# Order of the second maximum, the first sums and the outer stretches of values in a decode attention kernel

## The chip, the cores and the metric

The kernel runs on one core of a Trainium2 chip. The metric is the time of one execution on the device in microseconds (us). Before the change three runs took 639.89, 640.02 and 637.45 us; their median is 639.89. A separate execution was taken with the hardware profiler.

## What is computed

Grouped-query attention for a single query position: 32 query heads share 8 key/value heads (4 each), with 65536 keys of 128 numbers, all bf16.

```python
B, Hq, Hkv, Sq, Sk, D = 1, 32, 8, 1, 65536, 128
scores = jnp.einsum("bhqd,bhkd->bhqk", q, k) * scale
p = _softmax(scores, axis=-1)
return jnp.einsum("bhqk,bhkd->bhqd", p, v)
```

K and V are 134 MB each and every element is used once, so the kernel has to bring 268 MB into the core.

## The kernel before, in words

**Rounds.** The keys of one head are cut into two rounds of 32768 keys; 8 heads make 16 rounds (`NR`). A round's keys lie as 128 partitions times 256 rows: a "row" is a tile of 128 keys by 128 numbers. K of a round goes to `kbuf`, V to `vbuf`, each by one large transfer of 8 MB on SP's queue (`load_both`, L466). `kbuf` has room for 352 rows, so that the next round's keys can be written where this round's first part has been used up; `vbuf` holds one round.

**Parts.** Each round is worked on in two parts, a first part of 160 rows (`A`) and a second of 96 (`C`). Each part has a running maximum of its own, so there are 32 parts with indices `u`; `u % 2` tells first from second. In even rounds the first part is rows 0 to 160; in odd rounds it is rows 96 to 256 (`row_tile`, L63), so that the rows used first are those which the next load overwrites first.

**One round, engine by engine.**
- TensorE (`pe_keys`, L162) transposes the keys in blocks of 8 rows (L136) and multiplies each transposed block with the 4 queries (L155). The first part's scores go to two PSUM banks, the second part's to a third. The second part's transposes stand twice in the code, once for even and once for odd rounds, behind branches (L168, L171). Then `pe_values` (L181) multiplies the exponentials with V (L178) in three stretches of rows: 96 to 160 (stretch 1, in the first part of every round), 0 to 96 (stretch 0) and 160 to 256 (stretch 2). They are run in the order 1, 0, 2 with one wait for the semaphore `exd` ahead of stretch 1 (first part's exponentials) and one ahead of stretch 0 (second part's). The last round has code of its own (`pe_last`, L192), where the first part's 160 values stand ahead of the second wait.
- VectorE (`dve_round`, L321) and ScalarE share the copies of the transposed blocks from PSUM to `ktb` (L240, L238). VectorE then reduces the scores to a maximum per query (L260), GpSimd takes it over the partitions (L438), VectorE joins it with the running maximum (`maximum`, L276: `m`, `dm`, `negm`), and ScalarE computes the exponentials with their sums (`exponentials`, L390). `add_sums` (L287) adds these sums to `lp`; it waits for ScalarE (`sx`). In `dve_round` the first part's `add_sums` stands ahead of the second part's reduction.
- `add_values` (L307) waits for `pvd`, which TensorE sends with the last value, gives `vbuf` free (`vfree`), and adds the three stretches to `acc`.
- SP (`sync_engine`, L446) waits for `kfree`, queues the next K, waits for `vfree`, queues the next V. `kfree` comes from VectorE with the copy of the first part's last block (L236). All transfers are on one queue.

**The ends.** Up to round 13 K and V come in one transfer each, but for round 0's K in three. Round 14's K and V come in two (160 and 96 rows), round 15's K in three (64, 96 and 96 rows), each with a semaphore of its own (`krdy`), and round 15's V in eight: 96 and 64 rows for the first part, then 48, 24, 12, 6, 4 and 2 rows (`V_PIECES`) for the second. In `pe_last` a small matmul (L206) stands between the 48th and the 49th value of the second part and waits for VectorE's sums (`t_lp`, L377).

TensorE's program is a loop over the rounds (L222) whose start is aligned to a block of 256 instructions.

Of the kernel before, what the change touches and what calls it, by code (L numbers as in the profile page):

```python
# [5 lines left out]
DT = mybir.dt  # L6
AF = mybir.ActivationFunctionType
ALU = mybir.AluOpType
AX = mybir.AxisListType

P = 128


T = 128
C = 96
A = 2 * T - C
# [25 lines left out]
def take(e, sem, n=1):  # L42

    e.wait_ge(sem, n)
    e.sem_inc(sem, -n)  # L45


def bass_standalone__gqa_softmax__decode_kernel(nc, q, k, v, out):
    _, Hq, _, D = q.shape
    _, H, Sk, _ = k.shape  # L50
    R = Hq // H
# [3 lines left out]
    scale = float(D) ** -0.5  # L55
# [7 lines left out]
    def row_tile(odd, x):  # L63
        return (x + C) % (2 * T) if odd else x
# [6 lines left out]
    def sb(name, shape, dt):  # L71
        return S(nc.sbuf_tensor(name, shape, dt))

    def sem(name):
        return S(nc.semaphore(name))
# [14 lines left out]
    cmax = [sb(f"cmax{i}", [P, R], DT.float32) for i in range(2)]  # L90
    cmaxa = sb("cmaxa", [P, R], DT.float32)
    m = [sb(f"m{i}", [P, R], DT.float32) for i in range(2)]
    dm = sb("dm", [P, R], DT.float32)
    negm = sb("negm", [P, R], DT.float32)
    alpha = [sb(f"alpha{i}", [P, R], DT.float32) for i in range(2)]
    rsum = [sb(f"rsum{i}", [P, R], DT.float32) for i in range(2)]
    acc = sb("acc", [P, R], DT.float32)[:, :]
    lp = sb("lp", [P, R], DT.float32)
    la = sb("la", [P, R], DT.float32)
# [10 lines left out]
    pvb = S(nc.psum_tensor("pvb", [P, BANK], DT.float32))  # L110
# [3 lines left out]
    vrdy = [sem(f"vrdy{i}") for i in range(2)]  # L114
# [3 lines left out]
    qkd, qrdy, pvd = sem("qkd"), sem("qrdy"), sem("pvd")  # L118
    cm, cma, ng, exd, sx, lrd, lra = (sem(n) for n in ("cm", "cma", "ng", "exd", "sx", "lrd", "lra"))
    xd, xa, xg = sem("xd"), sem("xa"), sem("xg")  # L120
# [56 lines left out]
    def value(pe, out, r, first, last):  # L177
        return pe.matmul(out, lhsT=vbuf[:, r * D:(r + 1) * D], rhs=pts[:, r * R:(r + 1) * R],  # L178
                         start=first, stop=last)

    def pe_values(pe):  # L181

        for q, (a, b) in ((1, (C, A)), (0, (0, C)), (2, (A, 2 * T))):
            if q in (1, 2):
                take(pe, vrdy[q - 1], 16)
            if q in (1, 0):
                take(pe, exd)
            for r in range(a, b):
                ins = value(pe, pvb[:, q * R:(q + 1) * R], r, r == a, r == b - 1)
        ins.then_inc(pvd, 1)  # L190

    def pe_last(pe):  # L192
        starts = [sum(V_PIECES[:i]) for i in range(len(V_PIECES))]
        take(pe, exd)
        pe.wait_ge(t_o, H - 1)
        pe.transpose(qkb[0][0:HR - R, 0:P], oT[:, R:HR], identf[:, :]).then_inc(s_o, 1)
        for x in range(A):
            ins = value(pe, pvb[:, 0:R], row_tile(True, x), x == 0, x == A - 1)
            if x in (0, C):
                ins.wait_op(vrdy[x // C], 16, "sem-ge")  # L200
        ins.then_inc(pvd, 1)
        take(pe, exd)
        for r in range(C):
            if r == starts[1]:
                pe.wait_ge(t_lp, 1)
                pe.matmul(fin[0:R, P:P + 1], lhsT=lp[:, :], rhs=ones[:, :],  # L206
                          start=True, stop=True).then_inc(s_l, 1)
            ins = value(pe, pvl[:, 0:R], r, r == 0, r == C - 1)
            if r in starts:
                ins.wait_op(vpiece[starts.index(r)], 16, "sem-ge")  # L210
        ins.then_inc(pvd, 1)
        ins = pe.transpose(fin[0:R, 0:P], acc, identf[:, :])  # L212
        ins.wait_op(t_acc, 1, "sem-ge")
        ins.then_inc(s_fin, 1)

    def tensor_engine(pe):
        pe.wait_ge(q_sem, 16)
        pe.wait_ge(t_id, 1)
        pe.transpose(trb[0][:, 0:HR], qsb[:, :], ident[0:HR, 0:HR]).then_inc(s_x, 1)
        pe.wait_ge(t_qT, 1)  # L220
        pe.addr_align(256, offset=LOOP_SLOT, max_nops=16)
        with pe.Fori(0, NR) as i:  # L222
            pe_keys(pe, i)
            with pe.If(i < NR - 1):
                pe_values(pe)
        pe_last(pe)


# [15 lines left out]
    def own(e, ins, s):  # L244
        ins.then_inc(s, 1)
        take(e, s)
# [29 lines left out]
    def maximum(e, u):  # L276
        take(e, cma)
        mn, mo = m[u % 2], m[(u - 1) % 2]
        if u % HU == 0:
            e.tensor_copy(mn[:, :], cmaxa[:, :])  # L280
            e.tensor_scalar(negm[:, :], cmaxa[:, :], -scale, None, ALU.mult).then_inc(ng, 1)
        else:
            own(e, e.tensor_tensor(mn[:, :], mo[:, :], cmaxa[:, :], ALU.max), xd)  # L283
            e.tensor_tensor(dm[:, :], mo[:, :], mn[:, :], ALU.subtract)  # L284
            e.tensor_scalar(negm[:, :], mn[:, :], -scale, None, ALU.mult).then_inc(ng, 1)

    def add_sums(e, u):  # L287

        take(e, sx)
        if u % HU == 0:  # L290
            own(e, e.tensor_copy(lp[:, :], rsum[0][:, :]), xd)  # L291
        else:
            own(e, e.tensor_tensor(lp[:, :], lp[:, :], alpha[u % 2][:, :], ALU.mult), xd)  # L293
            own(e, e.tensor_tensor(lp[:, :], lp[:, :], rsum[0][:, :], ALU.add), xd)  # L294
        if u % 2 == 0:
            own(e, e.tensor_tensor(lp[:, :], lp[:, :], rsum[1][:, :], ALU.add), xd)
        if u % HU == HU - 1:
            e.sem_inc(lrd, 1)

    def rescale(e, u):  # L300
        if u % HU:
            own(e, e.tensor_tensor(acc, acc, alpha[u % 2][:, :], ALU.mult), xd)  # L302
# [4 lines left out]
    def add_values(e, i):  # L307

        rescale(e, 2 * i)
        take(e, pvd)  # L310
        e.sem_inc(vfree, 1)
        for n, q in enumerate((1, 2, 0) if i else (0, 1, 2)):
            pv = pvb[:, q * R:(q + 1) * R]
            if n == 2:
                rescale(e, 2 * i + 1)
            if i == 0 and n == 0:
                own(e, e.tensor_copy(acc, pv), xd)  # L317
            else:
                add(e, pv)

    def dve_round(e, i, h):  # L321

        a, b = 2 * i, 2 * i + 1
        evictions(e, 0, GA)
        first_part_done(e)
        evictions(e, GA, G - NTB)
        maximum(e, a)
        evictions(e, G - NTB, G)
        add_sums(e, a)
        largest(e, 2, C, cmax[0]).then_inc(cm, 1)  # L330
        pair_done(e, i)
        maximum(e, b)
        add_sums(e, b)
        if i < HALVES - 1:
            add_values(e, i)
        else:
            with e.If(h < H - 1):
                add_values(e, i)
                next_output(e)
# [22 lines left out]

    def vector_engine(e):
        identities(e)
        e.memset(dm[:, :], 0.0)
        own(e, e.memset(oT[:, :], 0.0), xd)
        e.wait_ge(s_x, 1)
        own(e, e.tensor_copy(qT[:, :], trb[0][:, 0:HR]), xd)
        next_queries(e, t_qT)
        e.sem_inc(qrdy, 1)  # L370
        with e.Fori(0, H) as h:
            for i in range(HALVES):
                dve_round(e, i, h)
        rescale(e, NU - 2)
        take(e, pvd)
        add(e, pvb[:, 0:R])
        e.sem_inc(t_lp, 1)  # L377
        rescale(e, NU - 1)
        e.wait_ge(s_o, 1)
        e.tensor_copy(orow[:, :], qkb[0][0:HR - R, 0:P]).then_inc(t_row, 1)  # L380
        e.wait_ge(s_l, 1)
        own(e, e.reciprocal(rl[:, :], fin[0:R, P:P + 1]), xd)
        ins = e.tensor_tensor(acc, acc, pvl[:, 0:R], ALU.add)  # L383
        ins.wait_op(pvd, 1, "sem-ge")
        ins.then_inc(t_acc, 1)
        ins = e.tensor_scalar(olast[:, :], fin[0:R, 0:P], rl[:, 0:1], None, ALU.mult)  # L386
        ins.wait_op(s_fin, 1, "sem-ge")
        ins.then_inc(t_last, 1)

    def exponentials(e, u):  # L390


        take(e, ng)
        e.activation(alpha[u % 2][:, :], dm[:, :], AF.Exp, scale=scale)  # L394
        pv = pts[:, :].rearrange("p (t g) -> p g t", g=R)
        for x, n, sums in ((A, C, 0),) if u % 2 else ((0, T, 0), (T, A - T, 1)):
            bank, t = scores(x)
            sv = bank[:, :].rearrange("p (t g) -> p g t", g=R)
            r = row_tile(u // 2, x)
            for g in range(R):  # L400
                ins = e.activation(pv[:, g, r:r + n], sv[:, g, t:t + n], AF.Exp,  # L401
                                   bias=negm[:, g:g + 1], scale=scale,
                                   accum_out=rsum[sums][:, g:g + 1])
        own(e, ins, xa)
        e.sem_inc(exd, 1)
        e.sem_inc(sx, 1)

    def act_round(e, i):
# [126 lines left out]
```

## Time and profile before

| what | value |
|---|---|
| median of three runs | 639.89 us (637.45 to 640.02) |
| the profiled execution | 641.53 us |
| its span, first to last instruction | 639.7 us |
| mean granted TensorE clock | 0.771 |
| read from HBM | 268.44 MB, 420 GB/s over the span |

PE is TensorE's matmul, PEld its weight load, DVE VectorE, ACT ScalarE, POOL GpSimd and SP the engine that queues the transfers. In a timeline row stand the start and the duration in us, the engine and line, the operation with its output and input, how often it comes in a row, and in brackets the idle time of that engine before it with what ended it. An ending in "q L45" names the engine's own sequencer in the helper `take` (L42), that is a wait for a semaphore; "issue" is time in which the engine waited for nothing that the profile shows.

### The profile page before, as it was taken

The numbers are of one execution on the slowest core, as the hardware profiler recorded it, in microseconds if no ns is written. First come the engines' busy times: TensorE is split into PE (matmuls) and PEld (weight loads), VectorE is DVE, ScalarE is ACT, GpSimd is POOL, SyncE is SP. The second block draws the span as 40 slices with busy tenths as digits, with TensorE's granted clock in tenths as the row PEclk, the third lists the DMA queues.
The fourth block names the chain that finished last, engine by engine and source line by source line (L and its number), as shares of the span: only waits on it lengthen the run. The fifth ranks groups of instructions, "written<-read, shape, count | busy, mean of one in ns | idle before, by whom it ended". The sixth has DMA issues, their size and how long they took to land. (4 is left out here: it accounts for less than half of the span.)

```text
span 639.7 us, 27108 instructions
## 1 busy us (share of the span) xinstructions
PE 484.3 (76%) x12293; PEld 477.2 (75%) x12293; DVE 311.0 (49%) x740; ACT 214.7 (34%) x562; POOL 16.4 (3%) x50
## 2 busy tenths in 40 slices
PE   4842977959778596876959759497694976979797
PEld 3842977959778596876959759497694976879796
DVE  4710744617356182552826427264372744638273
ACT  2420341504415143250523515135151351525243
POOL 0000000000000000000000000000000000000000
PEclk9965976959669596795958769588695876969696
DMA  9999999999999999999999999999999999999994
GB/s 375 465 412 428 443 418 414 451 418 438 434 414 430 426 438 422 406 443 422 434 434 410 430 426 443 414 422 422 426 430 426 426 434 418 421 417 423 434 425 182
DMA packets 6590, 268.63 MB, mean 420 GB/s; under 512 B 818, under 2 KB 1202, under 8 KB 1458
## 3 DMA queue, kind: packets, MB, share of 16 engines
q1 hardware_dynamic: 6488, 268.44, 98.2%
q8 instruction: 9, 0.15, 0.1%
q10 hardware_dynamic: 90, 0.02, 0.0%
q14 instruction: 3, 0.02, 0.0%
HBM read 268.44 MB, written 0.01 MB: 420 GB/s over the span
## 5 line engine op out<-in xcount | busy, mean ns | idle before, releaser
L136 PE MATMUL trb<-ident,kbuf 128*128 128x128 bf16 x4096 | 304.2, 232 | 73.0 <-PEq L45 71.6
L136 PEld LDWEIGHTS trb<-ident,kbuf 128*128 128x128 bf16 x4096 | 258.5, 104 | 74.7 <-issue 74.6
L240 DVE COPY ktb<-trb 128x1024 bf16<-128x1024 bf16 x368 | 243.5, 689 | 126.8 <-PE trb L136 122.9
L238 ACT ACTIVATE ktb<-trb 128x1024 bf16<-128x1024 bf16 x144 | 147.5, 1024 | 362.7 <-PE trb L136 356.2
L178 PE MATMUL pvb<-pts,vbuf 128*128 128x4 bf16 x4000 | 110.6, 166 | 64.2 <-PEq L45 61.5
L178 PEld LDWEIGHTS pvb<-pts,vbuf 128*128 128x128 bf16 x4000 | 108.9, 103 | 66.0 <-issue 65.9
L155 PE MATMUL qkb<-qcur,ktb 128*128 128x4 bf16 x4096 | 149.4, 165 | 8.9 <-issue 5.3
L155 PEld LDWEIGHTS qkb<-qcur,ktb 128*128 128x128 bf16 x4096 | 136.8, 97 | 12.0 <-issue 5.4
L401 ACT ACTIVATE pts<-qkb,negm 128x128 bf16<-128x128 f32 (+2 forms) x192 | 63.3, 460 | 0.0
L401 ACT ACTIVATION_READ_ACCUMULATOR pts<-qkb,negm 128x1 f32 x192 | 48.1, 255 | 0.0
L293 DVE TENSOR_TENSOR lp<-lp,alpha 128x4 f32<-128x4 f32 x24 | 3.9, 162 | 53.8 <-DVEq L45 53.8
L260 DVE TENSOR_REDUCE cmax<-qkb 128x4 f32<-128x512 f32 (+2 forms) x48 | 23.9, 510 | 7.9 <-DVEq L45 7.9
L438 POOL PARTITION_ALL_REDUCE cmaxa<-cmax x32 | 11.9, 372 | 589.7 <-POOLq L45 589.7
L394 ACT ACTIVATE alpha<-dm 128x4 f32<-128x4 f32 x32 | 6.4, 201 | 54.8 <-ACTq L45 54.8
L305 DVE TENSOR_TENSOR acc<-acc,pvb 128x4 f32<-128x4 f32 x38 | 6.0, 157 | 36.0 <-DVEq L45 31.6
L317 DVE COPY acc<-pvb 128x4 f32<-128x4 f32 x8 | 1.3, 162 | 44.8 <-DVEq L45 44.8
L291 DVE COPY lp<-rsum 128x4 f32<-128x4 f32 x8 | 1.4, 170 | 22.2 <-DVEq L45 22.2
L283 DVE TENSOR_TENSOR m<-m,cmaxa 128x4 f32<-128x4 f32 x24 | 3.8, 159 | 7.8 <-DVEq L45 7.8
L302 DVE TENSOR_TENSOR acc<-acc,alpha 128x4 f32<-128x4 f32 x24 | 3.9, 162 | 5.3 <-DVEq L45 3.1
L294 DVE TENSOR_TENSOR lp<-lp,rsum 128x4 f32<-128x4 f32 x24 | 3.9, 162 | 3.5
L284 DVE TENSOR_TENSOR dm<-m 128x4 f32<-128x4 f32 x24 | 3.9, 162 | 3.5
L440 POOL PARTITION_ALL_REDUCE la<-lp x8 | 3.5, 433 | 28.3 <-POOLq L45 28.3
(46 smaller groups left out, 34.5 us busy)
## 6 DMA issues: line engine op xcount, KB each, us to landing
kbuf<-in_k_dram SPq DMA_DIRECT2D x5, 3072.0 KB, 22.3
vbuf<-in_v_dram SPq DMA_DIRECT2D x2, 3072.0 KB, 20.4
kbuf<-in_k_dram SPq DMA_DIRECT2D x1, 5120.0 KB, 17.7
vbuf<-in_v_dram SPq DMA_DIRECT2D x1, 5120.0 KB, 17.3
kbuf<-in_k_dram SPq DMA_DIRECT2D x2, 2048.0 KB, 11.1
vbuf<-in_v_dram SPq DMA_DIRECT2D x1, 2048.0 KB, 21.2
vbuf<-in_v_dram SPq DMA_DIRECT2D x1, 1536.0 KB, 24.4
vbuf<-in_v_dram SPq DMA_DIRECT2D x1, 768.0 KB, 25.9
```

What stands on the lines that cost most here:

```text
L136: ins = pe.transpose(trb[j % NTB][:, i * P:(i + 1) * P], kbuf[:, t * D:(t + 1) * D], ident[:, :])
L155: ins = pe.matmul(bank[:, t * R:(t + 1) * R], lhsT=ktb[:, off:off + P], rhs=qcur[:, :], start=True, stop=True)
L178: return pe.matmul(out, lhsT=vbuf[:, r * D:(r + 1) * D], rhs=pts[:, r * R:(r + 1) * R], start=first, stop=last)
L238: ins = e.activation(dst, trb[j % NTB][:, :], AF.Copy).then_inc(eva, 1)
L240: ins = e.tensor_copy(dst, trb[j % NTB][:, :]).then_inc(evd, 1)
L260: return e.tensor_reduce(to[:, :], qkb[b][:, 0:n * R].rearrange("p (t g) -> p g t", g=R), AX.X, ALU.max)
L284: e.tensor_tensor(dm[:, :], mo[:, :], mn[:, :], ALU.subtract)
L293: own(e, e.tensor_tensor(lp[:, :], lp[:, :], alpha[u % 2][:, :], ALU.mult), xd)
L305: own(e, e.tensor_tensor(acc, acc, pv, ALU.add), xd)
L394: e.activation(alpha[u % 2][:, :], dm[:, :], AF.Exp, scale=scale)
L401: ins = e.activation(pv[:, g, r:r + n], sv[:, g, t:t + n], AF.Exp, bias=negm[:, g:g + 1], scale=scale, accum_out=rsum[sums][:, g:g + 1])
L438: e.partition_all_reduce(cmaxa[:, :], cmax[0][:, :], P, bass.bass_isa.ReduceOp.max).then_inc(cma, 1)
```

## The change

On VectorE the second part's reduction and `maximum` stand ahead of the first part's `add_sums`. As both parts' values are then alive together, `dm` and `negm` get two buffers and `rsum` three. On TensorE stretch 1 is followed by a loop of two passes; each pass waits for one count of `exd` and runs stretch 0 or stretch 2, chosen by the parity of round plus pass. ScalarE gives two counts of `exd` with the first part and one with the second. `pvd` is sent once per outer stretch, and VectorE waits for two.

```diff
-    rsum = [sb(f"rsum{i}", [P, R], DT.float32) for i in range(2)]
+    rsum = [sb(f"rsum{i}", [P, R], DT.float32) for i in range(3)]
...
-    def pe_values(pe):
-
-        for q, (a, b) in ((1, (C, A)), (0, (0, C)), (2, (A, 2 * T))):
-            if q in (1, 2):
-                take(pe, vrdy[q - 1], 16)
-            if q in (1, 0):
-                take(pe, exd)
-            for r in range(a, b):
-                ins = value(pe, pvb[:, q * R:(q + 1) * R], r, r == a, r == b - 1)
-        ins.then_inc(pvd, 1)
+    def stretch(pe, q):
+        a, b = ((0, C), (C, A), (A, 2 * T))[q]
+        for r in range(a, b):
+            ins = value(pe, pvb[:, q * R:(q + 1) * R], r, r == a, r == b - 1)
+        return ins
+
+    def pe_values(pe, i):
+
+
+        take(pe, vrdy[0], 16)
+        take(pe, exd)
+        stretch(pe, 1)
+        with pe.Fori(0, 2) as s:
+            take(pe, exd)
+            with pe.If((i + s) % 2 < 1):
+                stretch(pe, 0).then_inc(pvd, 1)
+            with pe.If((i + s) % 2 > 0):
+                take(pe, vrdy[1], 16)
+                stretch(pe, 2).then_inc(pvd, 1)
 
     def pe_last(pe):
         starts = [sum(V_PIECES[:i]) for i in range(len(V_PIECES))]
-        take(pe, exd)
+        take(pe, exd, 2)
...
     def add_values(e, i):
 
         rescale(e, 2 * i)
-        take(e, pvd)
+        take(e, pvd, 2)
...
         maximum(e, a)
         evictions(e, G - NTB, G)
-        add_sums(e, a)
         largest(e, 2, C, cmax[0]).then_inc(cm, 1)
         pair_done(e, i)
         maximum(e, b)
+        add_sums(e, a)
         add_sums(e, b)
...
-        for x, n, sums in ((A, C, 0),) if u % 2 else ((0, T, 0), (T, A - T, 1)):
+        for x, n, sums in ((A, C, 2),) if u % 2 else ((0, T, 0), (T, A - T, 1)):
...
-        e.sem_inc(exd, 1)
+        e.sem_inc(exd, 1 if u % 2 else 2)
         e.sem_inc(sx, 1)
```

More of the change, by code (lines that the diff above doesn't have):

```diff
@@ L92, in bass_standalone__gqa_softmax__decode_kernel @@
     m = [sb(f"m{i}", [P, R], DT.float32) for i in range(2)]
-    dm = sb("dm", [P, R], DT.float32)
-    negm = sb("negm", [P, R], DT.float32)
+    dm = [sb(f"dm{i}", [P, R], DT.float32) for i in range(2)]
+    negm = [sb(f"negm{i}", [P, R], DT.float32) for i in range(2)]
     alpha = [sb(f"alpha{i}", [P, R], DT.float32) for i in range(2)]
-    rsum = [sb(f"rsum{i}", [P, R], DT.float32) for i in range(2)]
+    rsum = [sb(f"rsum{i}", [P, R], DT.float32) for i in range(3)]
     acc = sb("acc", [P, R], DT.float32)[:, :]
@@ L224, in tensor_engine @@
             with pe.If(i < NR - 1):
-                pe_values(pe)
+                pe_values(pe, i)
         pe_last(pe)
@@ L280, in maximum @@
             e.tensor_copy(mn[:, :], cmaxa[:, :])
-            e.tensor_scalar(negm[:, :], cmaxa[:, :], -scale, None, ALU.mult).then_inc(ng, 1)
+            e.tensor_scalar(negm[u % 2][:, :], cmaxa[:, :], -scale, None, ALU.mult).then_inc(ng, 1)
         else:
             own(e, e.tensor_tensor(mn[:, :], mo[:, :], cmaxa[:, :], ALU.max), xd)
-            e.tensor_tensor(dm[:, :], mo[:, :], mn[:, :], ALU.subtract)
-            e.tensor_scalar(negm[:, :], mn[:, :], -scale, None, ALU.mult).then_inc(ng, 1)
+            e.tensor_tensor(dm[u % 2][:, :], mo[:, :], mn[:, :], ALU.subtract)
+            e.tensor_scalar(negm[u % 2][:, :], mn[:, :], -scale, None, ALU.mult).then_inc(ng, 1)
     def add_sums(e, u):
         take(e, sx)
+        first = rsum[2 if u % 2 else 0]
         if u % HU == 0:
-            own(e, e.tensor_copy(lp[:, :], rsum[0][:, :]), xd)
+            own(e, e.tensor_copy(lp[:, :], first[:, :]), xd)
         else:
             own(e, e.tensor_tensor(lp[:, :], lp[:, :], alpha[u % 2][:, :], ALU.mult), xd)
-            own(e, e.tensor_tensor(lp[:, :], lp[:, :], rsum[0][:, :], ALU.add), xd)
+            own(e, e.tensor_tensor(lp[:, :], lp[:, :], first[:, :], ALU.add), xd)
         if u % 2 == 0:
@@ L364, in vector_engine @@
         identities(e)
-        e.memset(dm[:, :], 0.0)
+        e.memset(dm[0][:, :], 0.0)
         own(e, e.memset(oT[:, :], 0.0), xd)
@@ L393, in exponentials @@
         take(e, ng)
-        e.activation(alpha[u % 2][:, :], dm[:, :], AF.Exp, scale=scale)
+        e.activation(alpha[u % 2][:, :], dm[u % 2][:, :], AF.Exp, scale=scale)
         pv = pts[:, :].rearrange("p (t g) -> p g t", g=R)
-        for x, n, sums in ((A, C, 0),) if u % 2 else ((0, T, 0), (T, A - T, 1)):
+        for x, n, sums in ((A, C, 2),) if u % 2 else ((0, T, 0), (T, A - T, 1)):
             bank, t = scores(x)
@@ L401, in exponentials @@
                 ins = e.activation(pv[:, g, r:r + n], sv[:, g, t:t + n], AF.Exp,
-                                   bias=negm[:, g:g + 1], scale=scale,
+                                   bias=negm[u % 2][:, g:g + 1], scale=scale,
                                    accum_out=rsum[sums][:, g:g + 1])
         own(e, ins, xa)
-        e.sem_inc(exd, 1)
+        e.sem_inc(exd, 1 if u % 2 else 2)
         e.sem_inc(sx, 1)
```

## The prediction, made before the changed kernel had run

> **What bounds the kernel now.** I read the page first: busy shares, then the transfer queue.
>
> ```profile
> span 639.7 us, 27108 instructions
> PE 484.3 (76%) x12293; PEld 477.2 (75%) x12293; DVE 311.0 (49%) x740; ACT 214.7 (34%) x562; POOL 16.4 (3%) x50
> q1 hardware_dynamic: 6488, 268.44, 98.2%
> L178 PE MATMUL pvb<-pts,vbuf 128*128 128x4 bf16 x4000 | 110.6, 166 | 64.2 <-PEq L45 61.5
> ```
>
> No compute engine is full, while the data queue (q1: packets, MB, share) fills 98.2% of the span on all 16 transfer engines. The missing 1.8% is 11.5 us. The last row, the values, is used further below (busy us, mean ns of one, idle us before them). Next I asked by stages where that lies (columns: stage, its length, busy us of PE, PEld, DVE, ACT, POOL, granted clock, DMA share, GB/s).
>
> ```profile
> 0.00:4.00 4.00, 0.00 (x0) 0.00 (x0) 2.33 (x16) 1.49 (x2) 1.01 (x10) 1.00 0.60 190
> 100.00:630.00 530.00, 416.99 (x10542) 411.53 (x10542) 266.72 (x614) 185.03 (x481) 12.62 (x33) 0.77 1.00 426
> 630.90:639.70 8.80, 5.73 (x187) 5.17 (x184) 2.06 (x13) 1.54 (x9) 0.54 (x2) 0.50 0.04 13
> ```
>
> The transfers run at 426 GB/s without a visible hole until about 631 us, then 8.8 us follow with almost none. So the kernel is a stream of 268 MB plus a tail of compute. A change can gain in two places only, the tail and small holes in the stream. For the middle I took the timeline of one round (round 7, counted from 0; odd and even rounds alternate).
>
> ```profile
> 279.97 2.54 PE L155 MATMUL qkb<-qcur,ktb 128*128 128x4 bf16 x96
> 283.68 1.77 PE L178 MATMUL pvb<-pts,vbuf 128*128 128x4 bf16 x64 [1.16 <-PEq L45]
> 284.49 0.56 DVE L260 TENSOR_REDUCE cmax<-qkb 128x4 f32<-128x384 f32 x1 [0.26 <-DVEq L45]
> 286.44 0.20 ACT L394 ACTIVATE alpha<-dm 128x4 f32<-128x4 f32 x1 [3.03 <-ACTq L45]
> 288.25 5.26 PE L178 MATMUL pvb<-pts,vbuf 128*128 128x4 bf16 x192 [2.79 <-PEq L45]
> 293.81 0.33 SPq L464 DMA_DIRECT2D vbuf<-in_v_dram  x1
> 298.14 1.12 PE L136 MATMUL trb<-ident,kbuf 128*128 128x128 bf16 x9 [4.64 <-PEq L45]
> ```
>
> The 64 middle values run, PE waits 2.79 us for the second part's exponentials, then 192 values run without a break to 293.51. Then the next load of V is issued (293.81), and PE waits 4.64 us for keys. That last wait ends with the landing of K, 4.3 us after V was queued, so the stream had its next transfer in hand. A shorter PE round there only lengthens PE's wait.
>
> The last rounds differ, because their keys are loaded in pieces and the first piece lands early. The first rows of the last three rounds on PE:
>
> ```profile
> 534.43 3.41 PE L136 MATMUL trb<-ident,kbuf 128*128 128x128 bf16 x32 [4.87 <-PEq L45]
> 568.78 3.31 PE L136 MATMUL trb<-ident,kbuf 128*128 128x128 bf16 x32
> 603.50 3.57 PE L136 MATMUL trb<-ident,kbuf 128*128 128x128 bf16 x32
> ```
>
> Round 13 still waits 4.87 us for keys. Rounds 14 and 15 start with no wait at all: from 534.43 to the end PE is one chain, and it is late against the stream. By how much, the landing times say (issue times in the second and last row, KB each, us from issue to landing):
>
> ```profile
> 548.35 0.81 SPq L459 DMA_DIRECT2D kbuf<-in_k_dram  x2
> kbuf<-in_k_dram SPq DMA_DIRECT2D x1, 5120.0 KB, 17.7
> L459 SPq DMA_DIRECT2D kbuf<-in_k_dram x3: 328/424/426, 583.6 to 584.5; - x3
> DMA to landing us min/median/max: 14.9/21.8/28.7
> L464 SPq DMA_DIRECT2D vbuf<-in_v_dram x8: 328/432/433, 603.8 to 607.0; - x8
> vbuf<-in_v_dram SPq DMA_DIRECT2D x1, 64.0 KB, 25.9
> ```
>
> Round 14's first keys landed at 548.35 + 17.7 = 566.05; PE came 2.7 us later. Round 15's three pieces landed at about 598.5, 605.8 and 613.2; PE came to the first 5.0 us late. The last piece of V landed at 607.0 + 25.9 = 632.9, and the last rows of the tail are far behind it:
>
> ```profile
> 610.55 0.61 PE L136 MATMUL trb<-ident,kbuf 128*128 128x128 bf16 x8
> 617.66 0.61 PE L136 MATMUL trb<-ident,kbuf 128*128 128x128 bf16 x8
> 625.06 2.54 PE L155 MATMUL qkb<-qcur,ktb 128*128 128x4 bf16 x96
> 628.87 4.40 PE L178 MATMUL pvb<-pts,vbuf 128*128 128x4 bf16 x160
> 629.88 0.56 DVE L260 TENSOR_REDUCE cmax<-qkb 128x4 f32<-128x384 f32 x1 [0.26 <-DVEq L45]
> 633.64 1.42 PE L178 MATMUL qkb<-pts,vbuf 128*128 128x4 bf16 x48 [0.38 <-PEq L45]
> 635.57 0.19 PE L206 MATMUL pvb<-ones,lp 128*4 128x1 f32 x2 [0.51 <-DVEq L377]
> 635.70 1.44 PE L178 MATMUL qkb<-pts,vbuf 128*128 128x4 bf16 x48
> 637.18 0.16 DVE L383 TENSOR_TENSOR acc<-acc,qkb 128x4 f32<-128x4 f32 x1 [0.67 <-PE qkb L178]
> ```
>
> The values end at 637.14, 4.2 us after their data was there. That lateness is what can be had.
>
> **The change part by part.** *Order of the outer stretches.* Today one wait stands ahead of both outer stretches of 96 values. After it, the one that belongs to the first part (rows 0 to 96 in even rounds, 160 to 256 in odd ones) runs behind the middle stretch, and only the other waits for the second exponentials. In the round shown, the values then run 283.68 + 1.77, 2.63 (half of 5.26) and 2.63. The second stretch ends at 288.08 and would itself be followed at once, since the exponentials' wait ended at 288.25 even without the other edit. So the whole wait of 2.79 us goes, and the cover is the first-part stretch.
>
> *The loop and its branches.* Each round gets a loop of two passes with two conditions in each, some of them jumps over 96 values. The nearest rows are the branches that the kernel has: the jump over the other copy of 96 transposes and the jump back at L222.
>
> ```profile
> 619.69 5.53 PE L136 MATMUL trb<-ident,kbuf 128*128 128x128 bf16 x96 [0.17 <-issue]
> ```
>
> That jump costs PE 0.17 us; at 568.78 and 603.50 the jump back costs no idle time, since the matmuls in hand cover it. With at most six taken or tested branches a round that is 0 to 1.0 us; I take 0.5, because the two loop passes meet more of them in a row than any row shows. Net per round: 2.79 - 0.5 = 2.3 us (1.8 to 2.8). What is behind PE, the `pvd` wait on VectorE, the release of V and its load, all come 2.3 us earlier. VectorE's wait for two counts instead of one costs nothing: both come in PE's order and the later one is the same event.
>
> *Second maximum ahead of the first sums.* On VectorE the reduction at 284.49 stood behind a wait for ScalarE's first part and two small sums; it now follows the scores, which end at 282.51. Its chain through GpSimd to ScalarE is 1.95 us (284.49 to 286.44), so the second exponentials start near 284.6 and not 286.44. In the round shown that is worth nothing beyond the other edit: PE is with the first-part stretch until 288.1. It gives cover, no time. The sums move behind it, into the time of the second exponentials, where VectorE idles. Three result slots instead of two and doubled small buffers cost no instruction.
>
> In the tail it does count, as the last round's order was right already. The reduction moves from 629.88 to about 627.75, just behind the scores (625.06 + 2.54); from it to PE's second part are 3.76 us (629.88 to 633.64), so PE could start at 631.5, but is busy until 628.87 + 4.40 = 633.27. Of the 0.38 us wait nearly all goes. The wait of 0.51 us at 635.57 is for a sum that VectorE can start late only because both sums were queued behind the second exponentials; these are 2 us earlier, so it goes too. Together 0.9 us (0.4 to 0.9).
>
> *What of it reaches the end.* Rounds 13 and 14 shorten by 2.3 us each, 4.6 in all. Round 14 then starts at 568.78 - 2.3 = 566.5, still behind its keys (566.05). Round 15 starts at 598.9 (keys 598.5), its ninth block comes at 610.55 - 4.6 = 605.95 (keys 605.8), and its last block of the first part at 617.66 - 4.6 = 613.06, where the keys land at 613.2: 4.4 us are left. With the tail's 0.9 the last values would end at 637.14 - 5.3 = 631.8. But the last V is there only at 632.9. So the transfer ends last: two matmuls (1.44/48 = 0.03 us each, 0.17 us for one to end by the page's row of L178) bring the end of the values to about 633.15, 4.0 us earlier. The rest of the tail is unchanged: span 635.7.
>
> *The stream itself.* With V queued earlier it has fewer holes.
>
> ```profile
> 178.00:180.00 2.00, 0.00 (x0) 0.00 (x0) 0.52 (x3) 0.00 (x0) 0.00 (x0) 0.50 0.96 360
> 256.00:258.00 2.00, 0.00 (x0) 0.00 (x0) 0.70 (x4) 0.00 (x0) 0.00 (x0) 0.50 1.30 426
> 413.00:416.00 3.00, 0.00 (x0) 0.01 (x1) 0.77 (x5) 0.00 (x0) 0.00 (x0) 0.50 1.02 371
> ```
>
> Some hand-overs from K to V run at 360 or 371 GB/s instead of 426: 0.31 and 0.39 us lost. Others show none. There are seven of that kind (each second round); two or so at 0.35 make 0.7 us, with bounds of 0 and 7 x 0.35 = 2.5. Everything behind shifts with the stream.
>
> *Sum.* 4.0 + 0.7 = 4.7 us. The profiled execution took 641.53 us with a span of 639.7, so 1.8 us lie around it; it would become 636.8. The median of the three runs is 639.89, 1.64 below the profiled one: 639.89 - 4.7 = 635.2.
>
> **The rivals.** *Only the tail counts.* If the chain of rounds 13 to 15 is less late in runs without a profile, the stream hides the shorter rounds, and 0.9 to 2 us remain: 637.9 to 639.0. For it: 13 rounds of 16 wait for keys anyway, and the lowest run, 637.45, is already 2.4 us below the median, as a run with half of the lateness would be. Against it: the rows at 568.78 and 603.50 without idle time, and two runs of three near 640. Chance 0.24.
>
> *Code that has to be loaded again.* The new loop jumps back over 192 values in every round. If its target is no longer at hand, PE stands still. The price is shown by the first round, where PE's code is loaded for the first time:
>
> ```profile
> 36.68 2.72 PE L155 MATMUL qkb<-qcur,ktb 128*128 128x4 bf16 x96 [5.27 <-issue]
> 50.84 2.92 PE L178 MATMUL pvb<-pts,vbuf 128*128 128x4 bf16 x104 [2.65 <-issue]
> PE qkb L155 <- issue: 5.3, 1, 5.3
> PE pvb L178 <- issue: 2.7, 1, 2.7
> ```
>
> Where PE's round grows by 5.27 - 2.3 = 3.0 us, V is queued 1.3 us before K lands instead of 4.3. Holes already show in the stream with leads like the 4.3 of round 7, so I price the new hole at what the lead loses, 4.3 - 1.3 = 3.0 us a round, 15 x 3.0 = 45, or 685 us; it decides from the point where the lead is used up. Against it: such a stall stands once per line in the list of waits, in the first round, though L222 jumps back over the whole body (864 matmuls and as many weight loads) fifteen times. The new body is larger by a handful of branch and register instructions only. Chance 0.05. [...]
>
> *Branches dearer than thought.* At 2.8 us or more a round they eat the wait; then only the tail's part is left or 1 to 3 us are lost: 639 to 643. Chance 0.05, half of it slower.
>
> **How the numbers follow.** The forecast, a tail bound by the last V, has 0.66: between 633.4 (all holes closed) and 636.9 (no holes closed, 1 us of PE still late). About 0.5% or 3.2 us is what a measurement of this kernel tells from no change. Faster than 636.7: nearly all of the forecast, 0.64. Within 3.2 us: the first rival, the forecast's edge and part of the last rival, 0.29. Slower: the code rival and half of the dear branches, 0.07. The range runs from 633.2 to 639.0 and takes in the first rival; the forecast's own is 633.4 to 636.9.
>
> **What would show it.** Right: the 2.79 us wait ahead of the second run of values is gone and VectorE's reduction of 384 follows the scores at once; V's loads are issued 2 us or more earlier against the landing of K; round 15 starts within 1 us of its keys (the wait on L136 is back); the last values wait for V's pieces, and the sum at L206 no longer waits. Wrong: idle time of PE from issue in every round (code), or more than 1 us between the stretches (branches), or a last round that starts as late as now.

## The result, and the profile after

The changed kernel takes 632.32 us (median of six runs, 631.43 to 632.61), the kernel before 640.3 us beside it (637.45 to 643.1). The ratio is 0.9869, with a 95% interval of 0.984 to 0.9897: 8.0 us or 1.3% faster. The forecast was 635.2 with 4.7 us of gain, the range 633.2 to 639.0. The direction was right, the size too small, and the time lies below the range.

The page of the changed kernel; the rows are those shown of before, and q8 is the queue that loads code:

```profile
span 630.7 us, 27318 instructions
PE 488.6 (77%) x12293; PEld 480.4 (76%) x12293; DVE 310.7 (49%) x740; ACT 214.9 (34%) x562; POOL 16.4 (3%) x50
q1 hardware_dynamic: 6488, 268.44, 98.7%
q8 instruction: 9, 0.15, 0.1%
```

The span fell by 9.0 us, though the engines do the same work. The stages (columns as in the prediction) tell where:

```profile
100.00:620.00 520.00, 421.35 (x10552) 414.88 (x10553) 267.41 (x619) 185.78 (x485) 13.02 (x34) 0.78 1.00 432
623.50:630.70 7.20, 3.68 (x113) 3.26 (x113) 1.25 (x6) 0.00 (x0) 0.00 (x0) 0.50 0.08 24
```

The DMA share of the middle is 1.00 as before, but 432 GB/s flow instead of 426. The stream that looked full was not at its rate. It shows in the spacing of the rounds, too. The first transposes of rounds 1 and 13 on PE start when keys land. Before, for round 1 (a row is cut off where the window asked for ends, so its duration and count can be short):

```profile
63.04 1.23 PE L136 MATMUL trb<-ident,kbuf 128*128 128x128 bf16 x10 [9.28 <-PEq L45]
```

After, for rounds 1 and 13:

```profile
62.96 1.33 PE L136 MATMUL trb<-ident,kbuf 128*128 128x128 bf16 x11 [7.52 <-PEq L45]
527.39 3.44 PE L136 MATMUL trb<-ident,kbuf 128*128 128x128 bf16 x32 [6.12 <-PEq L45]
```

Before, round 13 started at 534.43: twelve rounds of 39.28 us. After, they take 38.70 us each. That alone is 7.0 of the 9.0 us. The timeline of round 7 shows how the change came to it:

```profile
277.28 2.54 PE L155 MATMUL qkb<-qcur,ktb 128*128 128x4 bf16 x96
279.97 0.56 DVE L269 TENSOR_REDUCE cmax<-qkb 128x4 f32<-128x384 f32 x1 [1.69 <-DVEq L45]
280.99 4.52 PE L178 MATMUL pvb<-pts,vbuf 128*128 128x4 bf16 x160 [1.16 <-PEq L45]
281.93 0.21 ACT L404 ACTIVATE alpha<-dm 128x4 f32<-128x4 f32 x1 [1.21 <-ACTq L45]
283.21 0.26 ACT L411 ACTIVATION_READ_ACCUMULATOR pts<-qkb,negm 128x1 f32 x1
286.41 2.70 PE L178 MATMUL pvb<-pts,vbuf 128*128 128x4 bf16 x96 [0.90 <-PEq L45]
289.42 0.33 SPq L474 DMA_DIRECT2D vbuf<-in_v_dram  x1
```

The reduction follows the scores by 0.15 us, 160 values run in one piece, and the wait of 2.79 us has become one of 0.90 us. That rest is not the second exponentials: ScalarE was through with them at 283.47 (283.21 + 0.26), 2 us before the 160 values ended. What stands there in the code are the loop and its branches. V is issued 12.14 us after the scores began (289.42 - 277.28); before it was 13.84 us (293.81 - 279.97).

The end of the kernel: first rows of rounds 14 and 15, the issue of V's eight pieces with the landing of the last, and the last values.

```profile
560.12 2.19 PE L136 MATMUL trb<-ident,kbuf 128*128 128x128 bf16 x19 [0.50 <-PEq L45]
593.21 3.57 PE L136 MATMUL trb<-ident,kbuf 128*128 128x128 bf16 x32 [0.23 <-PEq L45]
618.58 3.99 PE L178 MATMUL pvb<-pts,vbuf 128*128 128x4 bf16 x146
624.84 0.53 PE L178 MATMUL pvb<-pts,vbuf 128*128 128x4 bf16 x14 [2.27 <-issue]
625.23 1.42 PE L178 MATMUL qkb<-pts,vbuf 128*128 128x4 bf16 x48
626.58 0.19 PE L215 MATMUL pvb<-ones,lp 128*4 128x1 f32 x2
626.70 1.44 PE L178 MATMUL qkb<-pts,vbuf 128*128 128x4 bf16 x48
```

```profile
L474 SPq DMA_DIRECT2D vbuf<-in_v_dram x8: 328/432/849, 593.2 to 596.5; - x8
vbuf<-in_v_dram SPq DMA_DIRECT2D x1, 64.0 KB, 28.6
```

The last V landed at 596.5 + 28.6 = 625.1, 7.8 us earlier than before (632.9). From there to the end are 5.6 us instead of 6.8. So 9.0 = 7.8 of the stream + 1.2 of the tail. And the tail has a stop that was not there before: 146 of 160 values, then 2.27 us in which PE waits for nothing that the profile shows ("issue"). V's rows for these values had all landed by 617.2 (landing records), so the stop is no wait for V.

### The profile page after: what moved, and what is told of

It reads as the page before. It is cut to its first block, busy times and chain, and to the rows that moved or that the text cites. A ratio compares the mean times of both kernels' runs of the same rounds, so it can differ in the third digit from the quotient of the medians.

```text
span 630.7 us, 27318 instructions
## 1 busy us (share of the span) xinstructions
PE 488.6 (77%) x12293; PEld 480.4 (76%) x12293; DVE 310.7 (49%) x740; ACT 214.9 (34%) x562; POOL 16.4 (3%) x50
## 3 DMA queue, kind: packets, MB, share of 16 engines
q1 hardware_dynamic: 6488, 268.44, 98.7%
## 5 line engine op out<-in xcount | busy, mean ns | idle before, releaser
L178 PE MATMUL pvb<-pts,vbuf 128*128 128x4 bf16 x4000 | 113.1, 166 | 37.9 <-PEq L45 31.1
L178 PEld LDWEIGHTS pvb<-pts,vbuf 128*128 128x128 bf16 x4000 | 110.3, 104 | 40.8 <-issue 40.3
```

## The experiments

**One edit at a time.** Theory (hand-over): V must be issued some time ahead of the end of K, else the stream loses at every change from K to V. The first kernel keeps TensorE's loop, and VectorE has its old order.

```diff
+        add_sums(e, a)
         largest(e, 2, C, cmax[0]).then_inc(cm, 1)
         pair_done(e, i)
         maximum(e, b)
-        add_sums(e, a)
```

> The changed kernel with VectorE's order as before (first part's sums ahead of the second part's reduction); TensorE's loop stays. Theory of the hand-over: a round takes the larger of 38.7 us (its transfers) and the time from the landing of K to the issue of V plus about 4.1 us. The loop alone takes about 2 us out of the second term, 35.2 to 33.2, so 38.7 decides: the landings of K stay 38.7 us apart and the time is within 1 us of the changed kernel's 632.3. Rival, the second maximum is what counts: it stays near before's 640.

Measured: 632.18 us (632.05 to 633.16), ratio to before 0.9857 (0.9841 to 0.9874). The second has VectorE's new order and TensorE's old one, without a loop.

```diff
-        with pe.Fori(0, 2) as s:
...
+        for q, n in ((1, 2), (0, 1), (2, 0)):
+            if q:
+                take(pe, vrdy[q - 1], 16)
+            if n:
+                take(pe, exd, n)
+            ins = stretch(pe, q)
+        ins.then_inc(pvd, 1)
...
-        take(e, pvd, 2)
+        take(e, pvd)
```

> The changed kernel with TensorE's old order of values (1, 0, 2 with one wait ahead of stretch 0) and no loop; VectorE's new order stays. Theory of the hand-over: the second exponentials are ready 1.9 us earlier, TensorE's 192 values follow that, V is issued 1.9 us earlier, 35.2 - 1.9 + 4.1 = 37.4 is below 38.7: 632 to 633.5, either edit alone is enough. Rival, the order of the stretches is what counts and the maximum gives only cover, as the prediction had it: near 639.

Measured: 632.78 us (632.53 to 634.65), ratio 0.9871 (0.9849 to 0.9892). Either edit alone brings the whole gain. So the gain isn't a sum of waits removed. It fits something that is reached once V comes about 2 us earlier (1.6 to 2.3 us against the issue of K in these two runs, rounds 2 to 13).

**V held back.** The changed kernel, with nothing but the issue of V delayed on SP in rounds 1 to 13, by n pairs of a semaphore count and a wait for it. By the issue times of rounds 2 to 13, n = 8, 16, 32, 48 and 64 put V off by 1.1, 2.1, 4.1, 6.1 and 8.3 us against the issue of K. They ran in the order 16, 8, 32, 64, 48:

```diff
+    late = sem("late")
...
             take(e, vfree)
+            for _ in range(n):
+                e.sem_inc(late, 1)
+                take(e, late)
             load_v(i, vrdy[0], 0, 2 * T)
```

> The changed kernel with every issue of V from round 1 to 13 held back on SP by 16 pairs of a semaphore count and a wait for it, about 2.4 us; nothing else is touched, and the last two rounds are not delayed. Theory of the hand-over: 33.1 + 2.4 + 4.1 = 39.6 us a round instead of 38.7, over 12 rounds 8 to 11 us: 640 to 643. Rival, a lead of 3 us hides the transfer all the same and the gain came from TensorE's chain in the last rounds: 632 to 633.

Measured: 640.9 us (639.46 to 642.05), ratio to before 0.9997 (0.9979 to 1.0014). With V late again the gain is gone, while all else of the change is in place. So TensorE's shorter chain in the last rounds can't have made the gain by itself. That the time before comes back so exactly is partly chance: by the landing records the last V lands at 636.4, 3.6 us later than before, and the tail behind it takes 3.4 us instead of 6.8.

> The changed kernel with V held back by 8 such pairs instead of 16, about 1.1 us. Theory of the hand-over: 33.1 + 1.1 + 4.1 = 38.3 us is still below 38.7, so nothing is lost: 632 to 633. Rival, every microsecond of lead counts in proportion (half of the loss of the 16 pairs): 636.

Measured: 632.67 us (631.33 to 635.03): 8 pairs cost nothing against the 632.32 us without them, 16 cost 8.6 us, so between these two lies a threshold.

> The changed kernel with V held back by 32 pairs, about 4.3 us. Theory of the hand-over: 33.1 + 4.3 + 4.1 = 41.5 us a round, 2.8 more than 38.7 over 12 to 13 rounds: 664 to 670. Rival, the loss is a fixed one of a late hand-over, some 0.7 us a round whatever the delay: 641.

Measured: 643.56 us, the median of nine runs from 640.52 to 649.79; a tenth took 651.11. This is far less than the rule said. The median is also above the 641 of a fixed loss, but the runs scatter widely, and the traced one is the fastest (640.52), which the fixed loss would fit. The trace holds 16 landing times of each transfer, one for each transfer engine. The table is worked out from them and from SP's issue times, for each hand-over from K to V (the change of the stream from a round's K to its V). It gives by how much V was issued ahead of the first engine that ended K, by how much ahead of the last one, and the loss: how much longer than 19.35 us V took to land after K, which is what it takes in the changed kernel (all in us; the runs with 64 and 48 pairs came later):

```
kernel, V of round        ahead of first   ahead of last   loss
before, 3 7 9 11          2.43 to 3.77     4.20 to 6.40    0.00 to 0.01
before, 5                 2.24             4.22            0.17
before, 13                2.48             4.42            0.31
before, 2 4 6 8 10 12     1.55 to 2.13     3.59 to 4.04    0.55 to 1.79
after, 2 to 12            3.86 to 4.79     5.16 to 6.06    0.00 to 0.01
8 pairs, 2 to 12          2.76 to 4.14     4.01 to 5.04    0.00 to 0.12
16 pairs, 2 to 12         1.68 to 2.95     3.60 to 5.13    0.00 to 1.34
32 pairs, even rounds     2.44 to 2.68     3.00 to 3.75    0.00 to 0.02
32 pairs, odd rounds 3-11 0.21 to 1.00     1.23 to 1.52    1.07 to 1.27
48 pairs, 2 to 12        -1.02 to 2.08    -0.20 to 2.82   -0.03 to 2.65
64 pairs, 2 to 7         -3.50 to 2.13    -2.51 to 2.84    0.01 to 5.17
64 pairs, 8 to 12        -0.64 to 0.24    -0.01 to 0.89    1.92 to 3.03
```

The column of the first engine sorts the hand-overs best: from about 2.4 us on at most 0.31 us is lost, and below it mostly more, the more is lacking. It is no sharp rule. Round 8 before lost 1.79 us with a lead of 2.13, round 4 of 64 pairs only 0.01 with the same lead. Rounds 7 and 10 of 48 pairs lost nothing behind K's last engine with leads of 0.33 and -0.26; there the engines ended K 2.5 and 2.7 us apart. The last engine sorts worse; 3.0 us ahead of it was enough with 32 pairs, 4.0 was not enough before. The engines ended K up to 2.7 us apart before, but only 0.4 to 1.1 us apart from round 2 on with 32 pairs. And late and timely rounds alternate there. This fits that a loss puts off the next K, so that the next V has that much more lead. In the kernel before, the losses of rounds 2 to 12 sum to 6.8 us, nearly the 7.0 us by which the rounds got shorter.

> The changed kernel with V held back by 64 pairs, about 7.8 us by the 0.12 us a pair that the earlier three showed. They also showed what decides: V must be issued 2.4 us ahead of the first of the 16 engines that ends K, not 4.1 ahead of the last, and after a late V the engines end within 0.5 us of each other instead of 2. So a round takes the larger of 38.7 and 33.1 + 7.8 + 2.4 + 0.5 = 43.8 us: 12 to 13 rounds at 5.1 us more, 692 to 702. Rival, a late V costs a fixed 1.1 us in each round at most, as the 32 pairs had it: 645 to 650.

Measured: 665.54 us (663.5 to 667.76), ratio 1.038 (1.0321 to 1.0438). The fixed loss is out. The larger-of rule gave too much again, as it leaves out the lead that a loss gives back (with 32 pairs 2.44 to 2.68 us in the even rounds, behind odd ones with 0.21 to 1.00). With it, by the author's estimate, the mean round would lie halfway between 38.7 us and the round that would give each V its full lead.

> The changed kernel with V held back by 48 pairs, about 5.9 us. Corrected rule, made from the 32 and 64 pairs: a V that is late costs what its lead to the first engine lacks of 2.4 us, but this puts off the next K by as much and gives the next V that lead, so that only about half of the lack is lost on the mean: rounds of (38.7 + 39.0 + 2.9)/2 = 40.3 us, 1.6 over 38.7 in 13 rounds, 632.3 + 21 = 653 (650 to 657). Rule before the correction, the larger of 38.7 and 39.0 + 2.9: 3.2 a round, 674. Rival, a fixed 1.1 us a round: 646.

Measured: 653.89 us (652.48 to 656.41), ratio 1.0225 (1.018 to 1.027), as the corrected rule said ahead of the run. For 32 pairs the same rule gives 642.7, 0.9 us below the median. For 16 pairs it gives no loss at all, 632.3, and 640.9 was measured: the rule counts 0.5 us for the spread of the engines, and with 16 pairs they ended K 1.8 to 3.0 us apart. So it describes the late runs, and no more.

**The same lead without the change.** The kernel before, with K of rounds 1 to 13 in two pieces, so that TensorE can start on the first:

```diff
-            load_k(i, odd)
+            load_k(i, odd, (0, 2))
             take(e, vfree)
```

> The kernel before, with K of rounds 1 to 13 loaded in two pieces (160 and 96 rows) as round 14's is; nothing of the change is in it. TensorE can start a round when the first piece is there, some 7 us before the rest, so that V is issued up to 7 us earlier against the landing of the whole K. Theory of the hand-over: the loss of the stream goes without the change, landings 38.7 us apart; TensorE's chain of some 34.5 us a round is not shorter, so the last rounds stay late: 633 to 635. Rival, the shorter round of TensorE is what counts: 639 to 641.

Measured: 632.66 us (631.5 to 633.34), ratio 0.985 (0.9819 to 0.9881). Its timeline on SP and on PE around the same round:

```profile
264.41 0.91 SPq L459 DMA_DIRECT2D kbuf<-in_k_dram  x2
284.44 0.33 SPq L464 DMA_DIRECT2D vbuf<-in_v_dram  x1
```

```profile
278.87 5.26 PE L178 MATMUL pvb<-pts,vbuf 128*128 128x4 bf16 x192 [0.48 <-PEq L45]
288.51 3.53 PE L136 MATMUL trb<-ident,kbuf 128*128 128x128 bf16 x32 [4.38 <-PEq L45]
```

V is issued at 284.44, 3.9 us before the first piece of K lands (288.37) and 11.2 us before the whole of it does (295.68; both by the landing records). The rounds are 38.8 us apart. TensorE's old order with its 192 values in one piece is untouched, and the whole gain is there. This shows it most plainly: it was the lead that was worth 8 us, not the order. Splitting K also makes its packets smaller (40 and 24 KB instead of 64, 8360 packets on q1 instead of 6488), but the changed kernel has the same rate without that (426 GB/s over the span, 425 with K in two pieces).

**The stop in the tail.** The last round's first-part values run on the loop's own code, so that the program behind the loop is shorter; VectorE adds two stretches there in place of one.

```diff
         with pe.Fori(0, 2) as s:
-            take(pe, exd)
             with pe.If((i + s) % 2 < 1):
-                stretch(pe, 0).then_inc(pvd, 1)
+                with pe.If(i + s < NR):
+                    take(pe, exd)
+                    stretch(pe, 0).then_inc(pvd, 1)
             with pe.If((i + s) % 2 > 0):
+                take(pe, exd)
                 take(pe, vrdy[1], 16)
                 stretch(pe, 2).then_inc(pvd, 1)
...
-        for x in range(A):
-            ins = value(pe, pvb[:, 0:R], row_tile(True, x), x == 0, x == A - 1)
...
-            with pe.If(i < NR - 1):
-                pe_values(pe, i)
+            pe_values(pe, i)
...
```

> The changed kernel with the last round's first-part values run by the loop's own code (stretches 1 and 2) and not by 160 further values of the last round, so that the program behind the loop is 320 instructions shorter; VectorE adds two stretches in place of one. Theory of the code block: the stop of 2.27 us in the last round's first-part values is the loading of the next 16 KB of code behind the transfers, and it goes with the code: the values end with the last piece of V, 2.3 to 2.8 us earlier, 629.5 to 630. Rival, the stop is a wait for V or for something else on TensorE: no change, 632.3.

Measured: 631.74 us (631.32 to 632.15), ratio 0.9849 (0.9832 to 0.9865). Its last values on PE:

```profile
617.87 1.85 PE L178 MATMUL pvb<-pts,vbuf 128*128 128x4 bf16 x64 [1.15 <-PEq L45]
619.99 2.70 PE L178 MATMUL pvb<-pts,vbuf 128*128 128x4 bf16 x96 [0.27 <-PEq L45]
623.71 0.39 PE L206 MATMUL qkb<-identf,oT 128*28 128x128 f32 x1 [1.01 <-issue]
623.89 1.47 PE L178 MATMUL qkb<-pts,vbuf 128*128 128x4 bf16 x48
625.41 1.44 PE L178 MATMUL qkb<-pts,vbuf 128*128 128x4 bf16 x48
```

The stop of 2.27 us is gone, as the theory of the code block said. The packet records agree: in the changed kernel a block of code is fetched from 622.24 to 623.32, and with the short end none is at that place. But stops of 0.27 and 1.01 us stand in its place, between its two stretches of values and behind the loop; that they are the loop's branches is not shown. So less than the expected 2.3 to 2.8 us came: the span is 1.3 us shorter (629.4), the median 0.6 us, and the runs of the two kernels overlap.

**Both together.** The short end and K in two pieces:

> The changed kernel with the short end of the earlier run and K of rounds 1 to 13 in two pieces. TensorE comes to round 14 with its work done, so it starts rounds 14 and 15 when their keys land (it was 1.4 and 2.9 us late) and the values end with the last V: 1.3 us less than with the short end alone, 630.0 to 630.8. Rival, the smaller transfers cost stream time or round 14 is late all the same: 631.7 or more.

Measured: 631.05 us (630.65 to 631.08), ratio to before 0.9829 (0.98 to 0.9858): a little over what was expected. Round 14 now starts 0.1 us after its keys land and round 15 0.9 us after (1.4 and 2.9 in the changed kernel), and the values end 0.6 us behind the last V. It is the fastest of all kernels here, 1.3 us below the changed one, whose runs lie between 631.43 and 632.61.

**More code in the loop.** The two orders as plain branches, with stretch 2 twice in the code:

```diff
-        with pe.Fori(0, 2) as s:
...
+        with pe.If(i % 2 > 0):
+            stretch(pe, 2).then_inc(pvd, 1)
+            take(pe, exd)
+        stretch(pe, 0).then_inc(pvd, 1)
+        with pe.If(i % 2 < 1):
+            take(pe, exd)
+            stretch(pe, 2).then_inc(pvd, 1)
```

> The changed kernel with the stretches behind plain branches instead of a loop: stretch 2 stands twice in the code, behind stretch 1 for odd rounds and behind stretch 0 for even ones. TensorE's loop over the rounds grows from about 1760 to 1945 instructions, from 7 to 8 blocks of 256. Theory one, 8 blocks stay at hand as 7 do: the branches ahead of the last stretch get cheaper, 631 to 633. Theory two, the fetch of the block behind the loop pushes the loop's first block out and code is loaded again in each round with a stop of 2 to 5 us, as in the first round: several blocks a round, 640 to 690.

Measured: 817.47 us (811.76 to 821.2), ratio 1.274 (1.2646 to 1.2835). The page's row of the code queue:

```profile
q8 instruction: 142, 2.33, 1.2%
```

and its list of waits on PE (us in total, times, longest):

```profile
PE pvb L178 <- issue: 96.1, 30, 6.3
PE trb L136 <- issue: 43.1, 16, 4.8
PE qkb L155 <- issue: 28.7, 8, 4.9
```

142 blocks of code of 16 KB each (2.33 MB) are loaded instead of 9, and in these three rows PE stands still for 168 us on "issue" (14 us in the same rows of the changed kernel). Of theory two this much holds: code is loaded again, with stops of up to 6.3 us. Its upper bound was still far too low, and what displaces the code is not shown. How many instructions a block has can be estimated here: twice 126 values lie between two stops (they start at 305.61 and 510.08 us), with their weight loads 252 instructions, near the 256 of the expectation.

## Why the prediction was off, point by point

- *What bounds the kernel.* "The transfers run at 426 GB/s without a visible hole" was the root of the error. The share of 1.00 was taken for the full rate. Where the transfer engines ran short between two transfers, they mostly showed as busy here, with longer packets: by the packet records a 64 KB packet takes 2.42 us in the median in both kernels, but of those between 380 and 420 us the slowest twentieth took 3.07 us or more before and 2.43 after. Most of the long ones start between 412 and 418 us, where the stream passes from K to V. The changed kernel's 432 GB/s at the same share shows what was missing.
- *The stream itself.* This is the step that failed: the term was 0.7 us, its bounds 0 to 2.5, and it measured 7.8 us (632.9 to 625.1 for the last V). The mechanism was named rightly, that V queued earlier closes holes from K to V in each second round. Its size was taken from two short windows at 0.35 us; the losses are 0.55 to 1.79 us in each even round (the table above), and those of rounds 2 to 13 sum to 7.1 of the 7.8 us.
- *Round 7's lead of 4.3 us "in hand".* The prediction measured against the landing of the last engine. To the first engine it was 2.49 us, just enough; the even rounds had 1.55 to 2.13. The round shown was one of those that lose nothing.
- *Order of the stretches, loop and branches.* The wait of 2.79 us was to go for 0.5 us of branches. It became 0.90 us, with 0.23 to 0.50 us more ahead of the next round, and V was issued 1.7 us earlier behind the scores (13.84 - 12.14) instead of the 2 us or more that the prediction named as a sign. Round 13 on PE took 32.73 us (560.12 - 527.39) instead of 34.35 (568.78 - 534.43): 1.6 us less, below the bounds of 1.8 to 2.8.
- *Second maximum.* "No time" beside the other edit was right (632.18 without it, 632.32 with it); alone it is worth as much as the loop.
- *What reaches the end.* 4.0 us were expected and 1.2 came. Rounds 14 and 15 start with idle times of 0.50 and 0.23 us, but these are no waits for keys: with the faster stream the keys had landed 1.4 and 2.9 us earlier, so TensorE stayed late. The last values didn't wait for V: TensorE stopped 2.27 us in the first-part values. Without that stop (short end) the values still ended 1.5 us behind V. The two errors pull in opposite ways, 7.1 us too little for the stream and 2.8 us too much for the tail; that the forecast of 635.2 came within 2.9 us of the time is partly luck.
- *Code that has to be loaded again.* The 5% were rightly small: the changed kernel loads 9 blocks, as before (seven up to 57.0 us, in the first round, and two from 622.2 us on, in the last). But the rival is real. One copy of 96 values more, and it costs 185 us rather than the 45 that it was priced at. Where the limit lies, the runs don't show: a loop of about 1760 instructions (by a count of the program) was not loaded again, one of about 1945 was, and nothing between them was tried.
- *Only the tail counts* was wrong, though in each round but the last two TensorE did wait for keys.

## What to carry to other kernels

A queue that shows as "100% busy" can still lose at its hand-overs, as here: look at the bytes per second (426 against 432 GB/s here, at the same share) and at the spacing of landings in equal rounds, and compare odd with even ones. Count the lead of the next transfer to the first engine that runs out, not to the landing of the whole. Where it falls short, more than one edit may bring it over the threshold; here three did, each with all of the gain, and a load in two pieces did as well as a new order of the work. Before a large loop is unrolled, count its instructions: here the step from about 1760 to about 1945 cost 185 us.

## What was not expected of the hardware

- V had to be issued about 2.4 us ahead of the first engine's end for next to nothing to be lost, though the first packet of a V issued into empty engines starts 0.97 us after the issue (64 pairs, by the packet records). What takes the rest of the 2.4 us, no run here shows.
- The 16 engines don't end a transfer together: up to 2.7 us apart in the kernel before, 0.4 to 1.1 us with 32 pairs, 1.8 to 3.0 us with 16. What brings them into step is open.
- A code block behind the loop cost 2.27 us of PE's time in the last round: it was fetched from 622.24 to 623.32 us, and PE ran on only at 624.84. In the kernel before it was fetched from 630.36 to 631.49 us, and PE ran its 160 values without a stop. That the transfers, which ran until 625.1, held up the later kernel's block is likely and not shown.
